# Operand splits in halves over six units, one transpose per unit, low parts of weights read back from DRAM

## The chip, the core and the metric

The kernel runs on one core of a Trainium2 chip. The metric is the device time of one execution in microseconds (us). Five engines work beside one another, each through its own instruction queue in order: TensorE (PE in the profile), VectorE (DVE), ScalarE (ACT), GpSimd (POOL) and SyncE (SP, which here only issues DMAs).

## What is computed

The reference is attention (8 heads, half with a local mask, half with a strided one), a top-2 mixture of experts, and a gated feed-forward block over 2304 tokens of width 512. The change touches the last block alone:

```
rms = sqrt(mean(x * x, axis=-1) + 1e-6)
xn  = x / rms * rms_g
g   = xn @ w_gate                      # 512 x 1536
out = (silu(g) * (xn @ w_val)) @ w_out # 1536 x 512
```

All of it is float32. The kernel makes a float32 product out of reduced-precision ones: an operand is split into a high part (a cast, on ACT) and a low part (operand minus high part, on DVE), and three matmuls are summed: high by high, high by low, low by high (`mm3`, lines 146 to 150).

## The kernel before

**Tiles and pairs.** The 2304 tokens are 18 tiles of 128 rows; six tiles make a pair p (two blocks of 384 tokens), so there are three pairs. The feed-forward width is cut into 12 columns f of 128. Columns 0 to 3 of pair 0 go through `plain` (line 1144) in a lead-in that a hand-written order at lines 1310 to 1361 sets. Everything else goes through `unit(n)` (line 1223), one for each (p, f): eight for pair 0 (f = 4 to 11), twelve for pair 1, twelve for pair 2.

**A unit** computes gate and value columns of both token blocks with seven block products (Strassen's scheme, Winograd's form) in place of eight. The seven activation operands A11, S2, S3, S1, A22, A12, S4 are split once per pair (`split_op`, line 1157); S1 to S4 are sums of blocks (`sums`, line 1164). The seven weight operands of a column lie in `uc` and `ud` in DRAM; `wload` (line 1176) loads those of unit n+2 and `wsplit` (line 1186) splits those of unit n+1, in four pieces, into the two halves of `BW`. TensorE's order within a unit is P1, P6, P7, P5, P4, P2, P3, each six matmuls of 384 columns, with the three output products `om` (three matmuls of 512 columns, line 1128) of each block of the unit before put between them. The products alternate between two PSUM banks (`nextb`, line 1117), so a product can't start before the product two places back has been read out: P1 by ACT's copy (line 1259), the others by DVE additions (lines 1265 to 1297). ACT does the silu (lines 1282, 1290) and the high part of h (line 1124), DVE the products and low parts.

**The next pair's tokens** come in while a pair runs. `fetch` (line 841) gathers the two expert rows of a tile on POOL's queue; `combine_parts` (line 849) gives four steps: weigh (ACT, line 855), add (DVE, line 858) with its square and sum (ACT, line 859), root (a tiny DVE step, line 862, and a power on POOL, line 863), and the normalising multiply (DVE, line 873). `tile_T` (line 1214) transposes the tile with four PE transposes (line 1219) into one of the two product banks, and ACT copies it to `xT` (line 1221). Lines 1227 and 1228 say in which unit a tile is fetched, combined and transposed: one or two tiles a unit, in units 3 to 8 or 4 to 9. A combine's steps stand behind P1, P6, P7 and P2; transposes stand before P5 and before P3. The sums S1 to S3 stand at the end of unit f = 9, S4 at the end of f = 10. `split_op` takes whole operands of 128x768, three in unit f = 10 and four in f = 11 (line 1245).

In each stage of a unit ACT's cast of a weight piece and DVE's subtraction that needs it are issued one behind the other (lines 1192 and 1193).

Of the kernel before, what the change touches and what calls it, by code (L numbers as in the profile page):

```python
# [9 lines left out]
F32 = mybir.dt.float32  # L10
# [14 lines left out]
def attn_moe_swiglu(ctx: ExitStack, tc: tile.TileContext, q, k, v, w_gate, w_noise, noise, w1, w2,  # L25
# [27 lines left out]
    yd = dram.tile([E * CAP + NOV * 128, DM], F32, name="yd")  # L53
    ud = dram.tile([18, 128, 1024], F32, name="ud")
    uc = dram.tile([NFC, 128, 1024], F32, name="uc")


    identf = keep.tile([128, 128], F32, name="identf")
# [782 lines left out]
    def fetch(t):  # L841
        YG[t] = []
        for kk in range(2):
            y = buf("yg")
            nc.gpsimd.indirect_dma_start(y, None, yd, bass.IndirectOffsetOnAxis(  # L845
                ap=posu[:, kk, t:t + 1], axis=0))
            YG[t].append(y)
# [19 lines left out]
    def combine(t):  # L867
        for part in combine_parts(t)[:3]:
            part()
# [258 lines left out]
    def om(p, f, i, t):  # L1128

        h = HG[p, f, i]  # L1130
        w = slot(cuse["O", f // 2])
        o = (f % 2) * 512
        b = ob[3 * i + t]
        mm3(b, h, w, (slice(t * 128, (t + 1) * 128),), (slice(o, o + 512),), f == 0, f == NFC - 1)
        if f == NFC - 1:
            y = buf("o")
            if t % 2 == 0:
                nc.scalar.copy(y, b)
            else:
                V.tensor_copy(y, b)  # L1140
            r = (p * 6 + i * 3 + t) * 128
            nc.sync.dma_start(out[r:r + 128, :], y)
# [11 lines left out]
        V.tensor_mul(sg, sg, pv_)  # L1154
        to_h(0, f, i, sg)()

    def split_op(p, n):
        src = {"A11": (0, 0), "A12": (0, 2), "A22": (1, 2)}.get(n)
        src = ST_[n] if src is None else xT[src[0]][:, src[1]:src[1] + 2]
        d = SOP[p, n]  # L1160
        nc.scalar.copy(d[:, 0], src)  # L1161
        V.tensor_tensor(d[:, 1], src, d[:, 0].bitcast(F32), op=OP.subtract)  # L1162

    def sums(*ns):
        a, b = xT
        a11, a12, a21, a22 = a[:, 0:2], a[:, 2:4], b[:, 0:2], b[:, 2:4]
        for n in ns:
            x, y, op = {"S1": (a21, a22, OP.add), "S2": (ST_["S1"], a11, OP.subtract),
                        "S3": (a11, a21, OP.subtract), "S4": (a12, ST_["S2"], OP.subtract)}[n]
            V.tensor_tensor(ST_[n], x, y, op=op)  # L1170


    cols = [(p, f) for p in range(NP) for f in range(NREG if p == 0 else 0, NFC)]
# [9 lines left out]
            nc.sync.dma_start(c, uc[f])  # L1183
            WS[n] = b, c

    def wsplit(n, i):
        if n < len(cols):
            d = BW[n % 2].rearrange("p s k n -> p s (k n)")
            b, c = WS[n]
            k0, k1, src = ((768, 1280, c[:, :512]), (0, 512, b[:, :512]), (1280, 1792, c[:, 512:]),  # L1190
                           (512, 768, b[:, 512:768]))[i]
            nc.scalar.copy(d[:, 0, k0:k1], src)  # L1192
            V.tensor_tensor(d[:, 1, k0:k1], src, d[:, 0, k0:k1].bitcast(F32), op=OP.subtract)  # L1193

    PROD = {"P1": ("A11", 0), "P2": ("A12", 1), "P3": ("S4", 2), "P4": ("A22", 6), "P5": ("S1", 5), "P6": ("S2", 3),
            "P7": ("S3", 4)}
# [17 lines left out]
    def tile_T(t):  # L1214
        ya, _ = X2.pop(t)
        turn["g"] += 1
        b = bank[(3, 6)[turn["g"] % 2]]
        for c in range(4):
            nc.tensor.transpose(b[:, c * 128:(c + 1) * 128], ya[:, c * 128:(c + 1) * 128], identf)
        o = (t % 3) * 128  # L1220
        nc.scalar.copy(xT[t // 3 % 2][:, :, o:o + 128], b.rearrange("p (c n) -> p c n", c=4))

    def unit(n):
        p, f = cols[n]
        pp_, pf = (p, f - 1) if f else (p - 1, NFC - 1)
        t6 = 6 * (p + 1)
        FETCH, COMB, TR = ({u: [k for k in range(6) if ([3, 3, 4, 5, 6, 7] if p else [4, 4, 5, 6, 6, 7])[k] + d == u] for u in range(NFC)}
                           if p + 1 < NP else {} for d in (0, 1, 2))
        trs = [t6 + k for k in TR.get(f, ())]
        wload(n + 2)  # L1230

        def om_(i, t):
            if (pp_, pf, i) in HG:
                om(pp_, pf, i, t)

        def tr():
            if trs:
                tile_T(trs.pop(0))

        def product(name):  # L1240
            b = nextb()
            prod(n, name, b)
            return b

        nxt = {NFC - 3: (), NFC - 2: ("A11", "S2", "S3"), NFC - 1: ("S1", "A22", "A12", "S4")}.get(f, ())
        nxt = [lambda x=x: split_op(p + 1, x) for x in nxt if p + 1 < NP]

        def next_op():
            if nxt:
                nxt.pop(0)()  # L1250

        cmb = [combine_parts(t6 + k) for k in COMB.get(f, ())]

        def comb():
            for c in cmb:
                c.pop(0)()

        b = product("P1")
        nc.scalar.copy(p1, b)
        comb()  # L1260
        LO.pop(0)()
        wsplit(n + 1, 0)
        om_(1, 0)
        b = product("P6")
        V.tensor_add(u2, b, p1)  # L1265
        wsplit(n + 1, 1)
        comb()
        om_(1, 1)
        b = product("P7")
        V.tensor_add(u3, b, u2)  # L1270
        wsplit(n + 1, 2)
        comb()
        om_(1, 2)
        tr()
        b = product("P5")
        V.tensor_add(sgb, b, u3)
        V.tensor_add(u2, b, u2)
        next_op()
        om_(0, 0)
        b = product("P4")  # L1280
        V.tensor_add(u3, b, u3)  # L1281
        nc.scalar.activation(u3, u3, AF.Silu)  # L1282
        wsplit(n + 1, 3)
        next_op()
        V.tensor_mul(sgb, sgb, u3)
        lo = to_h(p, f, 1, sgb)
        om_(0, 1)
        b = product("P2")
        V.tensor_add(sga, b, p1)
        nc.scalar.activation(sga, sga, AF.Silu)  # L1290
        lo()
        next_op()
        comb()
        om_(0, 2)
        tr()
        b = product("P3")
        V.tensor_add(u2, b, u2)  # L1297
        V.tensor_mul(sga, sga, u2)
        LO.append(to_h(p, f, 0, sga))
        next_op()  # L1300
        if p + 1 < NP:
            for k in FETCH.get(f, ()):
                fetch(t6 + k)
            if f == NFC - 3:
                sums("S1", "S2", "S3")
            if f == NFC - 2:
                sums("S4")


    advance(E * NF + 7)  # L1310
# [4 lines left out]
    plain(0, 1)  # L1315
    for t in range(3):
        om(0, 0, 0, t)
    plain(0, 2)
    combine(3)
    norm(3)  # L1320
    for t in range(3):
        om(0, 1, 0, t)
    combine(4)
    norm(4)
    plain(0, 3)
    x2_to_xt(3)
    combine(5)
    norm(5)
    for t in range(3):
        om(0, 2, 0, t)  # L1330
    x2_to_xt(4)
    om(0, 3, 0, 0)
    om(0, 3, 0, 1)
    x2_to_xt(5)
    om(0, 3, 0, 2)
    o_load(4)
    o_load(5)
    plain(1, 0)
    sums("S1", "S2")
    for h in range(2):  # L1340
        o_split(4, h)
    plain(1, 1)
# [1 line left out]
        o_split(5, h)  # L1344
    wload(0)
    wload(1)
    split_op(0, "S2")
    split_op(0, "S1")
    for t in range(3):
        om(0, 0, 1, t)  # L1350
    sums("S4", "S3")
    plain(1, 2)
    split_op(0, "S3")
    for t in range(3):
        om(0, 1, 1, t)
    for k in range(4):
        wsplit(0, k)
    plain(1, 3)
    split_op(0, "S4")
    for t in range(3):  # L1360
        om(0, 2, 1, t)
    LO = [lambda: None]
# [37 lines left out]
```

## Time and profile before

| | us |
|---|---|
| runs shown | 1126.36, 1126.59, 1130.0 |
| median | 1126.59 |
| profiled execution, time | 1129.92 |
| profiled execution, span of its trace | 1128.1 |

The profiled execution's own time is 1.8 us over its span, and 3.33 us over the median. Over the span PE is busy 94%, its weight loads 84%, DVE 66%, ACT 43%, POOL 20%; the 16 DMA engines move 148 GB/s on average. Attention and routing fill the first 200 us, the experts the time to 650 us, the lead-in of the last block 650 to 711 us, its units 711 to 1121 us. PE's busy time is to be read with care: matmuls overlap in the pipeline, and a matmul record of 384 columns lasts 0.34 us though the next one starts 0.17 us later.

### The profile page before, as it was taken

What the parts mean: (1) busy time and instruction counts of PE and PEld (TensorE: products, weight loads), DVE (VectorE), ACT (ScalarE), POOL (GpSimd) and SP (SyncE); (2) the same over time, 40 slices, a digit from 0 to 9 for tenths busy, and PEclk for the clock granted to TensorE, in tenths of its full rate; (3) what the DMA queues carried; (4) which work ended last, traced back from release to release, by engine and by line L of the source; (5) the groups of instructions that cost most, each with busy time, mean ns of one, the idle gap of its engine ahead of it and who ended that gap; (6) DMA issues with size and microseconds to landing.
All of it is one profiled execution on the core that took longest, in us unless ns stands there. A gap on an engine that the chain in (4) does not pass through costs nothing. (4 is left out here: it accounts for less than half of the span.)

```text
span 1128.1 us, 17700 instructions
## 1 busy us (share of the span) xinstructions
PE 1062.4 (94%) x6309; PEld 944.5 (84%) x6309; DVE 741.4 (66%) x1541; ACT 488.8 (43%) x1022; POOL 220.4 (20%) x261
## 2 busy tenths in 40 slices
PE   7988889999999999999999998989999999899998
PEld 5776767799999999988998897878889788799997
DVE  5675765358788888783552345666876767777675
ACT  4765752344444344432442334444444444443342
POOL 6555310303241414132100221021010110000000
PEclk8988989999999999999999998999999999999999
DMA  9967521468798899673641332232242332232211
GB/s 164 204 162 172 127 61 45 133 194 277 255 306 278 277 298 303 226 244 103 210 141 71 103 112 91 89 111 88 85 150 85 103 103 74 69 127 83 80 52 57
DMA packets 174810, 166.77 MB, mean 148 GB/s; under 512 B 66304, under 2 KB 134912, under 8 KB 174720
## 3 DMA queue, kind: packets, MB, share of 16 engines
q1 hardware_dynamic: 164656, 143.01, 40.9%
q0 software_dynamic: 9920, 22.35, 7.3%
q8 instruction: 50, 0.82, 0.3%
q14 instruction: 40, 0.33, 0.1%
q10 hardware_dynamic: 144, 0.26, 0.1%
HBM read 122.53 MB, written 42.99 MB: 147 GB/s over the span
## 5 line engine op out<-in xcount | busy, mean ns | idle before, releaser
L148 PE MATMUL bank<-xta,low 128*128 128x384 f32 x376 | 130.2, 346 | 12.0 <-DVE u L1270 4.2
L150 PE MATMUL bank<-xta,low 128*128 128x384 f32 x376 | 128.0, 340 | 0.0
L149 PE MATMUL bank<-xta,low 128*128 128x384 f32 x376 | 127.9, 340 | 0.0
L148 PE MATMUL bank<-ring,ha 128*128 128x512 f32 x288 | 114.6, 398 | 0.0
L150 PE MATMUL bank<-ring,ha 128*128 128x512 f32 x288 | 114.4, 397 | 0.0
L149 PE MATMUL bank<-ring,ha 128*128 128x512 f32 x288 | 114.2, 397 | 0.0
L148 PE MATMUL bank<-low 128*128 128x384 f32 x264 | 90.8, 344 | 10.8 <-DVE u L1270 4.3
L148 PEld LDWEIGHTS bank<-xta,low 128*128 128x128 f32 x376 | 71.8, 191 | 24.8 <-issue 6.9
L149 PE MATMUL bank<-low 128*128 128x384 f32 x264 | 89.9, 340 | 0.0
L150 PE MATMUL bank<-low 128*128 128x384 f32 x264 | 89.8, 340 | 0.0
L1029 POOL TENSOR_TENSOR dm<-dm,da 128x512 f32<-128x512 f32 x36 | 46.6, 1296 | 204.3 <-DVE da L1027 102.0
L161 ACT ACTIVATE ha<-bank 128x384 fp32r<-128x384 f32 x64 | 31.4, 490 | 123.1 <-PE bank L150 114.2
L162 DVE SCALAR_TENSOR_TENSOR ha<-bank,ha 128x384 fp32r<-128x384 f32 x64 | 35.5, 554 | 65.0 <-ACT ha L161 64.7
L149 PEld LDWEIGHTS bank<-xta,low 128*128 128x128 f32 x376 | 71.7, 191 | 4.3
L150 PEld LDWEIGHTS bank<-xta,low 128*128 128x128 f32 x376 | 71.5, 190 | 0.0
L1282 ACT ACTIVATE u<-u 128x384 f32<-128x384 f32 x32 | 16.8, 525 | 124.1 <-DVE u L1281 124.1
L148 PEld LDWEIGHTS bank<-low 128*128 128x128 f32 x264 | 49.6, 188 | 23.2 <-DVE u L1297 5.8
L845 POOL DMA_INDIRECT buf<-yd,posu x36 | 36.3, 1009 | 161.3 <-DMA yd<-buf 99.3
L150 PEld LDWEIGHTS bank<-ring,ha 128*128 128x128 f32 x288 | 54.1, 188 | 12.8 <-DVE ha L1126 0.6
L829 POOL DMA_INDIRECT buf<-xd,mapu x37 | 49.0, 1325 | 45.7 <-DVE posu L955 15.5
L148 PEld LDWEIGHTS bank<-ring,ha 128*128 128x128 f32 x288 | 54.2, 188 | 3.3 <-ACT ha L1124 0.5
L1193 DVE TENSOR_TENSOR low<-stage,low 128x512 fp32r<-128x512 f32 x64 | 39.5, 621 | 26.1 <-ACT low L1192 26.1
(284 smaller groups left out, 2828.9 us busy)
## 6 DMA issues: line engine op xcount, KB each, us to landing
stage<-in_moe_w_dram SPq DMA_DIRECT2D x128, 256.0 KB
yd<-buf SPq DMA_DIRECT2D x40, 256.0 KB
ud<-dm SPq DMA_DIRECT2D x36, 256.0 KB
stage<-uc SPq DMA_DIRECT2D x16, 512.0 KB
wc<-uc SPq DMA_DIRECT2D x16, 512.0 KB
yd<-zero SPq DMA_DIRECT2D x28, 256.0 KB
raw<-in_moe_w_gate_dram SPq DMA_DIRECT2D x12, 512.0 KB
raw<-in_moe_w_val_dram SPq DMA_DIRECT2D x12, 512.0 KB
```

Of the source, the lines that this page charges most:

```text
L148: nc.tensor.matmul(o, l[(slice(None), 0) + lsl], r[(slice(None), 0) + rsl], start=first, stop=False)
L149: nc.tensor.matmul(o, l[(slice(None), 0) + lsl], r[(slice(None), 1) + rsl], start=False, stop=False)
L150: nc.tensor.matmul(o, l[(slice(None), 1) + lsl], r[(slice(None), 0) + rsl], start=False, stop=last)
L161: nc.scalar.activation(h[:, 0], p, AF.Relu)
L162: nc.vector.scalar_tensor_tensor(h[:, 1], p, 0.0, h[:, 0].bitcast(F32), op0=OP.max, op1=OP.subtract)
L829: nc.gpsimd.indirect_dma_start(t, None, xd, bass.IndirectOffsetOnAxis(ap=mapu[:, e * NT + j:e * NT + j + 1], axis=0))
L845: nc.gpsimd.indirect_dma_start(y, None, yd, bass.IndirectOffsetOnAxis(ap=posu[:, kk, t:t + 1], axis=0))
L1029: nc.gpsimd.tensor_tensor(m, m, a.bitcast(F32), op=OP.add)
L1193: V.tensor_tensor(d[:, 1, k0:k1], src, d[:, 0, k0:k1].bitcast(F32), op=OP.subtract)
L1282: nc.scalar.activation(u3, u3, AF.Silu)
```

## The change

- `split_op` works on one half (128x384) and one part (high or low) at a time; `sums` works on a range of columns.
- `extras(p, f)` lays the next pair's splits and sums out over units f = 7 to 11 and f = 0 of the next pair. Within a unit they are taken one a stage, and a half's low part is issued one stage behind its high part.
- `wsplit` becomes `whi` and `wlo`. A piece's high part is cast one stage ahead of its subtraction; the first piece of unit n+2 is cast at the end of unit n.
- `wlo`: the first time that a column's weights are split, the low part (128x1792, 896 KB) is stored to a new DRAM tile `ul` by one DMA; in later pairs it is loaded from there by one DMA, and DVE does nothing for it. The columns 4 to 11 are stored in pair 0, 0 to 3 in pair 1: 12 stores, 20 loads.
- One tile a unit: fetched at f = 2 to 7, combined at f = 3 to 8, transposed at f = 4 to 9, with the transpose behind P1 and its `om`, before P6. The normalising multiply moves from behind P2 to behind P5.
- At the end of a pair other than the last, all six output copies are ACT's.
- In the lead-in, combines of tiles 3, 4 and 5 are moved forward and interleaved around `plain(0, 2)` and `plain(0, 3)`; fetches 6 and 7 and the combine of tile 6 are added to it.

```
+    ul = dram.tile([NFC, 128, 1792], F32, name="ul")
...
-            if t % 2 == 0:
+            if t % 2 == 0 or p + 1 < NP:
...
-    def split_op(p, n):
+    def split_op(p, n, h, part):
         src = {"A11": (0, 0), "A12": (0, 2), "A22": (1, 2)}.get(n)
-        src = ST_[n] if src is None else xT[src[0]][:, src[1]:src[1] + 2]
-        d = SOP[p, n]
-        nc.scalar.copy(d[:, 0], src)
-        V.tensor_tensor(d[:, 1], src, d[:, 0].bitcast(F32), op=OP.subtract)
-    def sums(*ns):
+        src = (ST_[n] if src is None else xT[src[0]][:, src[1]:src[1] + 2])[:, h]
+        d = SOP[p, n][:, :, h]
+        if part == 0:
+            nc.scalar.copy(d[:, 0], src)
+        else:
+            V.tensor_tensor(d[:, 1], src, d[:, 0].bitcast(F32), op=OP.subtract)
+    def sums(n, sl=slice(0, 384)):
         a, b = xT
-        a11, a12, a21, a22 = a[:, 0:2], a[:, 2:4], b[:, 0:2], b[:, 2:4]
-        for n in ns:
-            x, y, op = {"S1": (a21, a22, OP.add), "S2": (ST_["S1"], a11, OP.subtract),
-                        "S3": (a11, a21, OP.subtract), "S4": (a12, ST_["S2"], OP.subtract)}[n]
-            V.tensor_tensor(ST_[n], x, y, op=op)
+        a11, a12, a21, a22 = (x[:, c:c + 2, sl] for x in (a, b) for c in (0, 2))
+        x, y, op = {"S1": (a21, a22, OP.add), "S2": (ST_["S1"][:, :, sl], a11, OP.subtract),
+                    "S3": (a11, a21, OP.subtract), "S4": (a12, ST_["S2"][:, :, sl], OP.subtract)}[n]
+        V.tensor_tensor(ST_[n][:, :, sl], x, y, op=op)
...
-    def wsplit(n, i):
+    def whi(n, i):
-            k0, k1, src = ((768, 1280, c[:, :512]), (0, 512, b[:, :512]), (1280, 1792, c[:, 512:]),
-                           (512, 768, b[:, 512:768]))[i]
-            nc.scalar.copy(d[:, 0, k0:k1], src)
-            V.tensor_tensor(d[:, 1, k0:k1], src, d[:, 0, k0:k1].bitcast(F32), op=OP.subtract)
+            nc.scalar.copy(d[:, 0, slice(*PIECE[i])], (c[:, :512], b[:, :512], c[:, 512:], b[:, 512:768])[i])
+    def wlo(n, i):
+        if n < len(cols):
+            p, f = cols[n]
+            d = BW[n % 2].rearrange("p s k n -> p s (k n)")
+            b, c = WS[n]
+            sl = slice(*PIECE[i])
+            if (p and (p - 1, f) in cols):
+                if i == 0:
+                    nc.sync.dma_start(d[:, 1].bitcast(F32), ul[f])
+            else:
+                V.tensor_tensor(d[:, 1, sl], (c[:, :512], b[:, :512], c[:, 512:], b[:, 512:768])[i],
+                                d[:, 0, sl].bitcast(F32), op=OP.subtract)
+                if i == 3:
+                    nc.sync.dma_start(ul[f], d[:, 1].bitcast(F32))
...
+    def extras(p, f):
+        if p + 1 == NP:
+            return []
+        def halves(n):
+            return [(lambda h=h: split_op(p + 1, n, h, 0), lambda h=h: split_op(p + 1, n, h, 1)) for h in range(2)]
+        def part(n, k):
+            return None, lambda: sums(n, slice(k * 128, k * 128 + 128))
+        a11, s2, s3, s1, a22, a12, s4 = (halves(n) for n in ORDER)
+        s4s = [(None, lambda k=k: sums("S4", slice(k * 192, k * 192 + 192))) for k in range(2)]
+        return {7: [*a11, part("S1", 0), part("S2", 0), part("S3", 0)],
+                8: [part(n, 1) for n in ("S1", "S2", "S3")],
+                9: [part(n, 2) for n in ("S1", "S2", "S3")] + s2,
+                10: s3 + s4s, 11: s1 + a22 + [a12[0]], 12: [a12[1]] + s4}.get(f, [])
...
+        more = p + 1 < NP
+        ex = deque(extras(p, f) if f else extras(p - 1, NFC) if p else [])
+        todo = []
+        cmb = combine_parts(t6 + f - 3) if more and 3 <= f < 9 else []
...
+        def extra(k=1, last=False):
+            while todo:
+                todo.pop(0)()
+            for _ in range(0 if last else k):
+                if ex:
+                    hi, lo = ex.popleft()
+                    if hi is not None:
+                        hi()
+                    todo.append(lo)
...
         b = product("P1")
         nc.scalar.copy(p1, b)
         comb()
         LO.pop(0)()
-        wsplit(n + 1, 0)
+        wlo(n + 1, 0)
+        whi(n + 1, 1)
+        extra()
         om_(1, 0)
+        if more and 4 <= f < 10:
+            tile_T(t6 + f - 4)
         b = product("P6")
         V.tensor_add(u2, b, p1)
-        wsplit(n + 1, 1)
+        wlo(n + 1, 1)
+        whi(n + 1, 2)
         comb()
+        extra()
         om_(1, 1)
         b = product("P7")
         V.tensor_add(u3, b, u2)
-        wsplit(n + 1, 2)
+        wlo(n + 1, 2)
+        whi(n + 1, 3)
         comb()
+        extra()
         om_(1, 2)
-        tr()
         b = product("P5")
         V.tensor_add(sgb, b, u3)
         V.tensor_add(u2, b, u2)
-        next_op()
+        comb()
+        extra(2)
         om_(0, 0)
         b = product("P4")
         V.tensor_add(u3, b, u3)
         nc.scalar.activation(u3, u3, AF.Silu)
-        wsplit(n + 1, 3)
-        next_op()
+        wlo(n + 1, 3)
+        extra(last=True)
         V.tensor_mul(sgb, sgb, u3)
...
         V.tensor_add(sga, b, p1)
         nc.scalar.activation(sga, sga, AF.Silu)
         lo()
-        next_op()
-        comb()
         om_(0, 2)
-        tr()
         b = product("P3")
         V.tensor_add(u2, b, u2)
         V.tensor_mul(sga, sga, u2)
         LO.append(to_h(p, f, 0, sga))
-        next_op()
-        if p + 1 < NP:
-            for k in FETCH.get(f, ()):
-                fetch(t6 + k)
-            if f == NFC - 3:
-                sums("S1", "S2", "S3")
-            if f == NFC - 2:
-                sums("S4")
+        whi(n + 2, 0)
+        if more and 2 <= f < 8:
+            fetch(t6 + f - 2)
...
     for t in range(3):
         om(0, 0, 0, t)
-    plain(0, 2)
     combine(3)
     norm(3)
+    plain(0, 2)
+    c4, c5 = combine_parts(4), combine_parts(5)
+    c4.pop(0)()
+    c5.pop(0)()
+    c4.pop(0)()
+    x2_to_xt(3)
+    for c in (c5, c4, c5, c4, c5):
+        c.pop(0)()
     for t in range(3):
         om(0, 1, 0, t)
-    combine(4)
-    norm(4)
     plain(0, 3)
-    x2_to_xt(3)
-    combine(5)
-    norm(5)
+    x2_to_xt(4)
     for t in range(3):
         om(0, 2, 0, t)
-    x2_to_xt(4)
-    om(0, 3, 0, 0)
-    om(0, 3, 0, 1)
     x2_to_xt(5)
-    om(0, 3, 0, 2)
+    for t in range(3):
+        om(0, 3, 0, t)
     o_load(4)
     o_load(5)
+    fetch(6)
     plain(1, 0)
-    sums("S1", "S2")
+    sums("S1")
+    sums("S2")
     for h in range(2):
...
-    split_op(0, "S2")
-    split_op(0, "S1")
+    fetch(7)
+    for x in ("S2", "S1"):
+        for h in range(2):
+            for k in range(2):
+                split_op(0, x, h, k)
     for t in range(3):
         om(0, 0, 1, t)
-    sums("S4", "S3")
+    sums("S4")
+    sums("S3")
+    combine(6)
+    norm(6)
     plain(1, 2)
-    split_op(0, "S3")
+    for h in range(2):
+        for k in range(2):
+            split_op(0, "S3", h, k)
     for t in range(3):
         om(0, 1, 1, t)
-    for k in range(4):
-        wsplit(0, k)
+    for i in range(4):
+        whi(0, i)
+        wlo(0, i)
+    whi(1, 0)
     plain(1, 3)
-    split_op(0, "S4")
+    for h in range(2):
+        for k in range(2):
+            split_op(0, "S4", h, k)
     for t in range(3):
         om(0, 2, 1, t)
```

## Rows read from the trace of the kernel before

**Rows 1.** The page's first part: busy us, share of the span, instructions, by engine.
```profile
PE 1062.4 (94%) x6309; PEld 944.5 (84%) x6309; DVE 741.4 (66%) x1541; ACT 488.8 (43%) x1022; POOL 220.4 (20%) x261
```

**Rows 2.** ACT in order of time: P1's copy in nine units (start, length).
```profile
712.32 0.48 ACT L1259 COPY p<-bank 128x384 f32<-128x384 f32 x1 [1.24 <-PE bank L150]
...
723.81 0.48 ACT L1259 COPY p<-bank 128x384 f32<-128x384 f32 x1
...
796.22 0.47 ACT L1259 COPY p<-bank 128x384 f32<-128x384 f32 x1
...
825.61 0.47 ACT L1259 COPY p<-bank 128x384 f32<-128x384 f32 x1
...
871.73 0.48 ACT L1259 COPY p<-bank 128x384 f32<-128x384 f32 x1
...
952.74 0.47 ACT L1259 COPY p<-bank 128x384 f32<-128x384 f32 x1
...
982.36 0.47 ACT L1259 COPY p<-bank 128x384 f32<-128x384 f32 x1
...
1005.28 0.48 ACT L1259 COPY p<-bank 128x384 f32<-128x384 f32 x1
...
1016.88 0.48 ACT L1259 COPY p<-bank 128x384 f32<-128x384 f32 x1
```

**Rows 3.** PE's waits by releaser (us, times, longest): 712 to 826, then 826 to 983.
```profile
PE bank L148 <- DVE u L1270: 4.3, 4, 1.7
...
PE bank L148 <- DVE u L1270: 4.2, 5, 1.1
```

**Rows 4.** One combining unit of pair 1, by time: ACT, ACT, DVE, PE.
```profile
890.78 0.63 ACT L859 ACTIVATE buf<-buf 128x512 f32<-128x512 f32 x1 [2.01 <-issue]
...
891.41 0.60 ACT L1192 CAST low<-stage 128x512 fp32r<-128x512 f32 x1
...
892.05 0.69 DVE L1193 TENSOR_TENSOR low<-stage,low 128x512 fp32r<-128x512 f32 x1 [0.88 <-ACT low L1192]
...
891.22 0.44 PE L148 MATMUL bank<-xta,low 128*128 128x384 f32 x1 [1.07 <-DVE u L1270]
```

**Rows 5.** DVE groups from 712 to 1128: idle before them at the end.
```profile
L1126 DVE TENSOR_TENSOR ha<-sga,ha 128x384 fp32r<-128x384 f32 x32 | 17.8, 557 | 16.3 <-ACT ha L1124 16.2
L1162 DVE TENSOR_TENSOR xta<-sS,xta 128x768 fp32r<-128x768 f32 x5 | 4.8, 956 | 2.5 <-ACT xta L1161 2.5
```

**Rows 6.** The lead-in, DVE and PE: tile 5's normalising, its transposes, first unit.
```profile
682.43 0.75 DVE L873 SCALAR_TENSOR_TENSOR buf<-buf,ms,gB 128x512 f32<-128x512 f32 x1 [0.66 <-POOL ms L863]
...
683.23 0.66 PE L138 MATMUL bank<-identf,buf 128*128 128x128 f32 x4 [3.86 <-DVE buf L873]
...
711.05 0.33 PE L148 MATMUL bank<-xta,low 128*128 128x384 f32 x1
```

**Rows 7.** Windows: span, busy PE, PEld, DVE, ACT, POOL; clock; DMA share; GB/s.
```profile
689.00:691.00 2.00, 2.00 (x8) 2.00 (x8) 0.00 (x0) 0.49 (x1) 0.00 (x0) 0.50 0.31 104
...
871.73:952.74 81.01, 75.50 (x386) 66.55 (x385) 56.39 (x109) 36.16 (x80) 11.12 (x14) 1.00 0.29 95
...
1015.00:1016.00 1.00, 1.00 (x8) 1.00 (x7) 0.90 (x3) 0.02 (x1) 0.00 (x0) 1.00 0.95 349
1016.00:1017.00 1.00, 1.00 (x6) 0.86 (x6) 0.37 (x1) 0.54 (x2) 0.00 (x0) 1.00 0.64 229
```

**Rows 8.** PE in unit 9 of pair 1: a tile's four transposes, merged.
```profile
943.76 0.60 PE L1219 MATMUL bank<-identf,buf 128*128 128x128 f32 x4
```

**Rows 9.** Around P1's copy in a unit of pair 2: PE's first `om`, then ACT.
```profile
1004.39 0.39 PE L148 MATMUL bank<-ring,ha 128*128 128x512 f32 x1
...
1004.86 0.51 ACT L1124 CAST ha<-sga 128x384 fp32r<-128x384 f32 x1 [1.44 <-DVE sga L1298]
...
1005.65 0.62 ACT L1192 CAST low<-wc 128x512 fp32r<-128x512 f32 x1
```

**Rows 10.** SP's queue in time: the last weight load of a unit being issued.
```profile
1013.90 0.42 SPq L1183 DMA_DIRECT2D wc<-uc  x1
```

More of the change, by code (lines that the diff above doesn't have):

```diff
@@ L1184, in wload @@
             WS[n] = b, c
-    def wsplit(n, i):
+    PIECE = ((768, 1280), (0, 512), (1280, 1792), (512, 768))
+    def whi(n, i):
         if n < len(cols):
@@ L1226, in unit @@
         t6 = 6 * (p + 1)
-        FETCH, COMB, TR = ({u: [k for k in range(6) if ([3, 3, 4, 5, 6, 7] if p else [4, 4, 5, 6, 6, 7])[k] + d == u] for u in range(NFC)}
-                           if p + 1 < NP else {} for d in (0, 1, 2))
-        trs = [t6 + k for k in TR.get(f, ())]
+        more = p + 1 < NP
+        ex = deque(extras(p, f) if f else extras(p - 1, NFC) if p else [])
+        todo = []
+        cmb = combine_parts(t6 + f - 3) if more and 3 <= f < 9 else []
         wload(n + 2)
@@ L1234, in om_, with comb @@
                 om(pp_, pf, i, t)
-        def tr():
-            if trs:
-                tile_T(trs.pop(0))
+        def extra(k=1, last=False):
[7 more added lines that the diff above has]
+                    todo.append(lo)
+        def comb():
+            if cmb:
+                cmb.pop(0)()
         def product(name):
@@ L1243, in product @@
             return b
[L1245 to L1256, printed above, removed]
         b = product("P1")
```

## The prediction, made blind

> **What bounds it now.** I read the page's first part first: PE is busy 94% of the span [rows 1]. That is an average, and it says only that no other engine can be the bound for long. So I looked for the stretches in which PE is not paced by its own work, by taking P1's copy as a clock hand: its distance from one unit to the next is the length of a unit [rows 2]. In pair 2, where no next pair is prepared, a unit takes 1016.88 - 1005.28 = 11.60 us. Its matmuls move 42 x 384 + 18 x 512 = 25344 columns, so 0.458 ns a column; a product of six matmuls is then 1.06 us and one `om` 0.70. I take 11.60 as what PE alone costs.
>
> Against it, pair 0: the first unit (f = 4) 11.49, f = 5 to 9 together 72.41 (five units, 14.5 each), f = 10 and 11 29.39 (14.7 each). Pair 1: f = 0 to 3 46.12 (11.5 each), f = 4 to 9 81.01 (13.5 each), f = 10 and 11 29.62 (14.8 each) [rows 2]. So some 14 + 6 + 11 + 6 = 38 us lie over PE's pace, in just the units that prepare a pair, of which the transposes, priced below, are 12 x 0.60 = 7.2.
>
> The waits say why. The longest kind of PE wait in both pairs is for the DVE addition that reads P7, up to 1.7 us at a time [rows 3]. In a combining unit [rows 4] ACT sits for 2.01 us before the square, because that needs DVE's add; the cast of the third weight piece stands behind it in ACT's queue; DVE's subtraction of this piece then waits 0.88 us, and behind that stand the additions that free the banks. The reader should see a ring between two in-order queues, each waiting for the other within one stage. In f = 10 and 11 the whole-operand splits do the same: casts and subtractions of 128x768, the latter 0.96 us each [rows 5].
>
> [...]
>
> **The change, part by part.** Lead-in: tile 5's combine moves from behind `plain(0, 3)` to ahead of it. A `plain` is 24 x 384 columns, 4.2 us, more than the wait of 3.86; so the wait goes, and I take the clock's 3 us with it, as the clock fell behind that idle time alone: 6.9 us. Given back: the combine of tile 6 now stands in ACT's and DVE's queues ahead of `plain(1, 2)`'s multiply, which frees a bank; no row shows such a chain on the path there, so it costs between 0 (hidden by PE's work) and 4 us (all of its steps in series). One of its waits, 0.66 us for POOL [rows 6], is small, so I stay near the low end and take 1.2. **Lead-in: -5.7, bounds -7 to -2.5.**
>
> Units with a transpose: the ring is cut, since casts run one stage ahead of their subtractions and the square stands behind the next weight cast. DVE keeps up: it is busy 56.39 of 81.01 us in the worst stretch of pair 1 [rows 7], and from there on loses four subtractions a unit. What is new is the bank. With the transposes (0.60 us [rows 8]) behind P1, P6 takes P1's bank, not P3's, and must wait for P1's copy. In a clean unit [rows 2, 9] P1's slot ends at 1004.39 where `om` starts; ACT's cast of h follows at 1004.86 and the copy from 1005.28 to 1005.76, 1.37 behind P1. The change puts one more cast between them, the first weight piece of unit n+2: 0.62 long, 0.11 of it overlapped as for the copy (0.48 long, its successor 0.37 behind it). So the copy ends 1.88 behind P1. PE has 0.70 of `om` and 0.60 of transposes until then, 1.30: it waits 0.6, and 0.1 is lost as a matmul behind a wait lasts 0.44 [rows 4] in place of 0.34. I take 0.7 a unit; ends are 0 and 1.2 (the wait of 1.07 that such a unit has now [rows 4], and the restart). A unit with a transpose is 11.60 + 0.60 + 0.7 = 12.90. In f = 7 two casts of A11 stand ahead of ACT's copy of the transposes, which frees P7's bank: 0.3 more once a pair.
> Pair 0, f = 5 to 9: 5 x 12.90 + 0.3 = 64.8 against 72.41: **-7.6**. Pair 1, f = 4 to 9: 6 x 12.90 + 0.3 = 77.7 against 81.01: **-3.3**. Pair 0's f = 4 has half the `om` (20736 columns, 9.5 us) and is 2.0 over that now; it gains a transpose with its wait (1.3) and a combine, and I leave it at 11.5: **0**, bounds -1.5 to +1.5.
>
> Units f = 10 and 11: three and four operands of 128x768 become some five half-size pieces a unit, one a stage. Two halves cost DVE 2 x 0.56 against 0.96 [rows 5], 0.16 more for each of 14 operands, hidden in DVE's idle time. Nothing else is late there, and no transpose: 2 x 11.65 against 29.39 and 29.62, **-6.1 and -6.3**; at worst half of the excess stays, 6 us in all. The pieces that spill into f = 0, and the three output copies a pair that ACT takes from DVE, I cost at 0: ACT is busy 36.16 of 81.01 us [rows 7]; without that cover it is three copies of a 512-column bank, under 2 us a pair.
>
> Low parts in DRAM: 12 stores and 20 loads of 917 KB on SP's queue. A load for unit n+1 can't go before P3 of unit n-1 has read the buffer, and must be there for P1 of unit n+1, one unit later. The last weight DMA of a unit is issued at 1013.90 [rows 10]; its and its neighbour's 640 KB move at 349 and 229 GB/s and are through by 1017 [rows 7]. 917 KB at 229 GB/s are 4.0 us, about 5 from issue to landing; with the unit's 896 KB of other weight loads in the same stretch, 9. The unit hides either. The stores delay SP's next weight load to the last stages of the unit, still a unit ahead of its use. POOL's gathers are as many as before, one tile a unit. The normalising multiply now comes one product sooner behind POOL's power, 0 to 0.7 us a tile (the 0.66 above); I take 0, as two bank additions stand between. In pair 2 PE is already at its pace, so DVE's saved subtractions buy nothing: 0.
>
> Sum: -5.7 - 7.6 - 3.3 - 6.1 - 6.3 = -29.0. Against the profiled execution's own 1129.92 that is 1100.9. This execution is 3.33 over the median, and whether that excess is among the things that go isn't shown: with the median of 1126.59 the sum gives 1097.6. I forecast between them, **1099**.
>
> [...] PE now idles briefly at the same bank in 11 more or less equal units; the row of pair 1's f = 4 to 9, with waits of 1.07 in it, has the clock at 1.00 throughout [rows 7], so I cost the clock at nothing. [...]
>
> **Rivals.** *The bank wait doesn't appear*, since ACT gets to the copy sooner: 11 x 0.7 = 7.7 less, 1091. For it: ACT is mostly idle. Against: the cast of h before it waits for a DVE product that nothing moves. Chance 0.13.
> *Half the gain*: transposing units stay at 13.5 (11 x 0.6 = +6.6) and the lead-in gives only 2.5 (+3.2) because DVE, with two more steps in most stages, is late for P5's and P4's banks: 1109. For it: pair 0 still subtracts weights, and a stage gives 1.76 us. Chance 0.17.
> *Slower, low parts late*: P1 of each of 20 units waits for its load. Price: each us of landing over the 11.6 of a unit costs 20; it turns the result slower from 11.6 + 29/20 = 13.1 us on, and at 13.5 it costs 20 x 1.9 = 38, 9 more than the rest gives: 1136. For it: traffic of a unit doubles and the queue is in order. Against: 349 GB/s for a lone load [rows 7]. Chance 0.04.
> [...] Chance 0.02.
> *No effect*: the rings were not the cause, and what one engine no longer waits for the other does: 1127. Against: each wait in [rows 4] names its cause. Chance 0.03.
>
> **Numbers.** The forecast has 0.61. No change, within 0.3% (3.4 us, about what a measurement of this kernel can tell from none), has 0.03; slower 0.06; faster 0.61 + 0.13 + 0.17 = 0.91. The low end takes in most of the missing bank wait from the median, 1089; the high end the half gain and part of the bounds of f = 10 and 11, 1113. Outside is about 0.15.
>
> **What would show it.** Right: P1's copies 12.9 apart in transposing units and 11.6 to 11.7 in f = 10 and 11; a PE wait for ACT's P1 copy in each of the twelve transposing units, the largest kind that is left; no wait of 3.86 and clock 1.00 in the lead-in; the first unit's P1 near 705 where it is at 711.05 now [rows 6]; pair 2 at 11.60. Wrong: waits for the `ul` load, PE waits for DVE's additions of over 1 us, a clock of 0.50 among the units.

## The result, and the profile after

The changed kernel takes **1100.88 us** (median of four runs, 1100.13 to 1101.69); the kernel before, run beside it, 1126.92 (four runs, 1126.36 to 1130.0). The ratio is **0.9764 [0.9744, 0.9784]**. The forecast was 1099, range 1089 to 1113, with 0.91 on faster. The profiled execution took 1100.19, over a span of 1098.4.

The first part of the page after, to hold against [rows 1]:

```profile
PE 1051.4 (96%) x6309; PEld 944.9 (86%) x6309; DVE 700.1 (64%) x1489; ACT 494.5 (45%) x1044; POOL 223.1 (20%) x261
```

PE issues the same 6309 matmuls and is busy 11 us less, for the same work: a record behind a wait is longer (0.45 for 0.34, in the rows of E1 below), and so is one at a granted clock of 0.50 (0.52 for 0.34, from 687 to 691 us of the kernel before; 3.4 of the 11 us lie in the lead-in, in which PE was busy 52.18 and is now 48.81). So PE's busy time doesn't hold the answer; the distances between P1's copies do, as in [rows 2]. ACT after, in order of time:

```profile
704.61 0.47 ACT L1294 COPY p<-bank 128x384 f32<-128x384 f32 x1
...
716.85 0.47 ACT L1294 COPY p<-bank 128x384 f32<-128x384 f32 x1
729.79 0.47 ACT L1294 COPY p<-bank 128x384 f32<-128x384 f32 x1
742.74 0.47 ACT L1294 COPY p<-bank 128x384 f32<-128x384 f32 x1
...
781.83 0.47 ACT L1294 COPY p<-bank 128x384 f32<-128x384 f32 x1
...
851.42 0.47 ACT L1294 COPY p<-bank 128x384 f32<-128x384 f32 x1
...
929.33 0.47 ACT L1294 COPY p<-bank 128x384 f32<-128x384 f32 x1
940.93 0.47 ACT L1294 COPY p<-bank 128x384 f32<-128x384 f32 x1
952.52 0.47 ACT L1294 COPY p<-bank 128x384 f32<-128x384 f32 x1
```

P1's copies of units with a transpose are 12.94 and 12.95 apart (716.85, 729.79, 742.74), those of units f = 10 and 11 of pair 1 11.60 and 11.59. Before, units f = 5 to 8 of pair 0 and 4 to 8 of pair 1 took 13.6 to 17.7 (f = 9 12.1 and 11.7), units f = 10 and 11 14.3 to 15.4. From the first P1 copy to the last, over 31 units, the kernel before took 397.36 and the changed one 374.99: -22.4. The lead-in (its first plain silu to the first P1 copy) fell from 56.33 to 49.82: -6.5. Ahead of that, in code that the change doesn't touch, this execution is 1.2 shorter (654.79 against 655.98), and behind the last P1 copy 0.3 longer. Together -29.7, the difference of the two spans.

PE's waits after, 655 to 1099 us (us in all, times, longest):

```profile
PE bank L149 <- ACT p L1294: 7.2, 11, 0.8
PE bank L149 <- ACT u L1154: 0.7, 1, 0.7
```

The waits of [rows 3] for the addition that reads P7 are gone. What is left is mainly one kind: P6 waiting for P1's copy, eleven times, 0.65 each on the mean. That the ring is open is best seen on DVE. First the largest group of weight subtractions of the kernel before (704 to 1127 us), then the same group of the kernel after (704 to 1098); the last column is DVE's idle time just ahead of them and what ended it:

```profile
L1193 DVE TENSOR_TENSOR low<-stage,low 128x512 fp32r<-128x512 f32 x64 | 39.5, 621 | 26.1 <-ACT low L1192 26.1
```

```profile
L1208 DVE TENSOR_TENSOR low<-stage,low 128x512 fp32r<-128x512 f32 (+1 forms) x20 | 12.4, 620 | 0.0
```

Before, 26.1 us of DVE's idle time stood right in front of a subtraction of this group that waited for its own cast (with the other pieces it is 52.5); after, none in any group: the cast is a stage old. The instruction itself lasts 620 ns either way.

### The profile page after: what moved, and what is told of

Same layout as the page of the kernel before. It is cut to its first block, busy times and chain, and to the rows that moved or that the text cites. A ratio compares the mean times of both kernels' runs of the same rounds, so it can differ in the third digit from the quotient of the medians.

```text
span 1098.4 us, 17694 instructions
## 1 busy us (share of the span) xinstructions
PE 1051.4 (96%) x6309; PEld 944.9 (86%) x6309; DVE 700.1 (64%) x1489; ACT 494.5 (45%) x1044; POOL 223.1 (20%) x261
## 5 line engine op out<-in xcount | busy, mean ns | idle before, releaser
L846 POOL DMA_INDIRECT buf<-yd,posu x36 | 38.5, 1069 | 155.2 <-DMA yd<-buf 98.6
L151 PEld LDWEIGHTS bank<-ring,ha 128*128 128x128 f32 x288 | 54.0, 187 | 12.4 <-DVE ha L1127 0.3
L149 PEld LDWEIGHTS bank<-low 128*128 128x128 f32 x264 | 49.6, 188 | 15.7 <-ACT p L1294 9.8
L132 DVE TENSOR_TENSOR low<-stage,low 128x1024 fp32r<-128x1024 f32 x34 | 42.6, 1256 | 23.2 <-ACT low L131 21.4
```

The lines of the kernel that those rows point to most:

```text
L132: lo_engine.tensor_tensor(r[:, 1], st, r[:, 0].bitcast(F32), op=OP.subtract)
L149: nc.tensor.matmul(o, l[(slice(None), 0) + lsl], r[(slice(None), 0) + rsl], start=first, stop=False)
L151: nc.tensor.matmul(o, l[(slice(None), 1) + lsl], r[(slice(None), 0) + rsl], start=False, stop=last)
```

## The experiments

Each chip measured the kernel before anew (1122.87, 1125.89 and 1122.69 for the three groups that ran together), so kernels of different groups are compared by their ratios. "Units" is the time from the first P1 copy to the last in the profiled execution; it leaves out the first 650 us, which vary by up to 8 us from one profiled execution to another.

### E2: the low parts without DRAM

```diff
-            if (p and (p - 1, f) in cols):
-                if i == 0:
-                    nc.sync.dma_start(d[:, 1].bitcast(F32), ul[f])
-            else:
-                V.tensor_tensor(d[:, 1, sl], ...)
-                if i == 3:
-                    nc.sync.dma_start(ul[f], d[:, 1].bitcast(F32))
+            V.tensor_tensor(d[:, 1, sl], ...)
```

> The low parts of weights are made by DVE in every unit; the stores to ul and the loads from it are gone. Theory (DVE has room once casts run a stage ahead, so the DRAM copy buys nothing): 1100.9, units of pair 1 at 12.9 and 11.6 as now. Rival (DVE's 2.2 us a unit are needed in pair 1's units that prepare pair 2): those nine units are 0.3 to 1 us longer, 1104 to 1110.

Measured: 1097.2, ratio 0.976 [0.9735, 0.9785]; units 374.87 against 374.99. Part four of the change, 32 transfers of 896 KB, buys nothing here and costs nothing: DVE has room for all its subtractions once they need not wait. (At another place of the transposes it buys 2.2 us: E10.)

### E4: the ring closed again

E2's kernel with each cast back in the stage of its subtraction:

```diff
+        whi(n + 1, 0)
         wlo(n + 1, 0)
-        whi(n + 1, 1)
...
+        whi(n + 1, 1)
         wlo(n + 1, 1)
-        whi(n + 1, 2)
...
-        whi(n + 2, 0)
```

> Each weight piece is cast and subtracted in the same stage again, as before the change, DVE makes all low parts (no ul), and no cast stands ahead of P1's copy; transposes stay before P6, operands stay halved. Theory of the prediction (the ring of ACT and DVE within a stage was what made combining units long): the ten units with a combine are 13.2 us or longer although the bank wait is gone, the two with a transpose alone 12.4; 3 to 7 us slower than the changed kernel, ratio to the kernel before 0.979 to 0.983. Rival (the place of the transposes and their number a unit were the cause): all twelve at 12.3 to 12.5, 6 us faster, ratio 0.971.

Measured: 1108.96, ratio 0.9852 [0.9824, 0.9879]; units 384.02, 9.2 over E2. The size is above the 3 to 7 us that were expected, and it lies elsewhere. The ten units with a combine were to take 13.2 or longer; four do (f = 7 and 8, in which sums and splits share the queues), the other six are 12.83 to 12.88, no longer than the transposing units of the changed kernel, and f = 9, with a transpose alone, is 13.28 and not 12.4. Unit f = 3 of pair 1 shows the ring by itself, with a combine and no transpose: 12.87 where E2 has 11.59. ACT's P1 copies of f = 7 and 8 of pair 0, then those around f = 3 of pair 1, and PE's waits of 655 to 1140 us:

```profile
744.33 0.47 ACT L1287 COPY p<-bank 128x384 f32<-128x384 f32 x1
...
759.43 0.47 ACT L1287 COPY p<-bank 128x384 f32<-128x384 f32 x1
...
772.95 0.47 ACT L1287 COPY p<-bank 128x384 f32<-128x384 f32 x1
...
844.91 0.47 ACT L1287 COPY p<-bank 128x384 f32<-128x384 f32 x1
...
857.78 0.47 ACT L1287 COPY p<-bank 128x384 f32<-128x384 f32 x1
```

```profile
PE bank L148 <- ACT ha L1124: 7.2, 10, 1.4
PE bank L148 <- ACT p L1287: 3.7, 11, 0.4
```

Units f = 7 and 8 are 15.10 and 13.52. With one cast fewer ahead of P1's copy, the bank wait halves (3.7 us in all for 7.2), and that pays for part of the ring: what the changed kernel doesn't have is PE waiting for ACT's cast of h, late behind the weight casts. So the two parts of the change pull against each other at this place, which led to the next two.

### E1: the extra cast ahead of P1's copy moved away

```diff
         nc.scalar.activation(sga, sga, AF.Silu)
+        whi(n + 2, 0)
         lo()
...
         LO.append(to_h(p, f, 0, sga))
-        whi(n + 2, 0)
```

> The first weight piece of unit n+2 is cast behind the second silu, ahead of the cast of h, in place of behind it; nothing else differs. Theory (P6 waits for its bank because this cast delays P1's copy by 0.52 us): the copy ends 1.37 us behind P1 and not 1.89, the PE wait for it shrinks from about 0.6 to 0.1 us, a transposing unit goes from 12.94 to 12.4 us, twelve of them give 6.5 us: 1094.4. Rival (the copy waits for the chain of DVE and ACT steps of h in any case, or DVE is what paces these units): 12.9 stays, 1100.9.

Measured: 1090.45, ratio 0.9708 [0.9683, 0.9732]; units 369.64, 5.35 less. Transposing units are 12.42 to 12.43, three of them 12.68 to 12.71. ACT and PE around P6 in the changed kernel:

```profile
728.85 0.51 ACT L1125 CAST ha<-sga 128x384 fp32r<-128x384 f32 x1 [1.95 <-DVE sga L1338]
729.27 0.61 ACT L1195 CAST low<-wc 128x512 fp32r<-128x512 f32 x1
729.79 0.47 ACT L1294 COPY p<-bank 128x384 f32<-128x384 f32 x1
...
729.08 0.60 PE L1237 MATMUL bank<-identf,buf 128*128 128x128 f32 x4
730.31 0.45 PE L149 MATMUL bank<-low 128*128 128x384 f32 x1 [0.64 <-ACT p L1294]
```

and in E1:

```profile
724.28 0.51 ACT L1125 CAST ha<-sga 128x384 fp32r<-128x384 f32 x1 [1.73 <-DVE sga L1339]
724.70 0.47 ACT L1294 COPY p<-bank 128x384 f32<-128x384 f32 x1
...
724.23 0.60 PE L1237 MATMUL bank<-identf,buf 128*128 128x128 f32 x4
725.23 0.44 PE L149 MATMUL bank<-low 128*128 128x384 f32 x1 [0.40 <-ACT p L1294]
```

With the cast between them gone, the copy starts 0.42 behind the cast of h (724.28, 724.70) in place of 0.94 (728.85, 729.79), and a unit is 0.5 shorter. The prediction's bank wait is shown by its cause. It isn't gone: the copy still ends after the transposes.

### E5: the transposes ahead of P5

```diff
-        if more and 4 <= f < 10:
-            tile_T(t6 + f - 4)
         b = product("P6")
...
         om_(1, 2)
+        if more and 4 <= f < 10:
+            tile_T(t6 + f - 4)
         b = product("P5")
```

The sums and halves that need a tile begin two stages later.

> The transposes stand before P5 again (one tile a unit), and the sums and splits are moved on by up to two stages so that they stay behind them. Theory (before, P5 waited there because DVE was late with P7 through the ring with ACT; with the casts a stage ahead it is in time, and P6 no longer shares P1's bank): no bank wait, 12.3 us a transposing unit, 7 us less: 1094. Rival (the place itself costs the wait, whatever DVE does): 13.3 to 13.6 a unit, 1106 to 1109.

Measured: 1087.3, ratio **0.9686 [0.9655, 0.9718]**; units 366.48, 8.5 less than in the changed kernel. Three P1 copies of pair 1, and PE's longest kind of wait from 690 to 1090 us:

```profile
844.21 0.47 ACT L1295 COPY p<-bank 128x384 f32<-128x384 f32 x1
...
856.25 0.46 ACT L1295 COPY p<-bank 128x384 f32<-128x384 f32 x1
...
868.28 0.47 ACT L1295 COPY p<-bank 128x384 f32<-128x384 f32 x1
```

```profile
PE bank L149 <- DVE u L1310: 0.8, 2, 0.6
```

12.04 and 12.03 a unit (in pair 0 mostly 12.4: see E10): the transposes cost 0.44 over the 11.60 of a unit without them, and the wait for P1's copy is gone from the list. The place that the kernel before had, ahead of P5, is the better one once the ring is cut; what it is worth with the ring closed is the next question.

### E10 and E11: is it the place or the ring?

E10 is E5 without the low parts in DRAM (E2's edit); E11 is E10 with casts and subtractions in one stage (E4's edit).

> Transposes before P5 with casts a stage ahead, and DVE makes all low parts (no ul). In the run with ul, pair 0's combining units (DVE subtracts there) took 12.4 and pair 1's (it doesn't) 12.04. Theory (that 0.37 is DVE's subtractions, hidden behind the bank wait in the changed kernel): pair 1's five combining units go to 12.4, 2 us more than with ul. Rival (pair 0's excess comes from something else, such as the stores): pair 1 stays at 12.04.

> As the run before it, but with the transposes before P5, where they stood before the change (one tile a unit): against the run with transposes before P5 and casts a stage ahead (12.0 to 12.4 a unit) it differs in the weights' casts and in ul alone. Theory (ring): the wait for P7's addition is back, 13.3 to 13.6 in the ten combining units, as units f = 6 to 8 had before the change; about 10 us slower than that run, ratio 0.977 or so. Rival (one tile a unit and halved operands are enough): 12.5 or less, ratio 0.970.

Measured: E10 1093.73, ratio 0.9711 [0.9682, 0.974]; E11 1107.72, ratio 0.9832 [0.9802, 0.9862]. With E2 and E4 they fill a square, all without the low parts in DRAM (units, us):

| | cast one stage ahead | cast in its stage |
|---|---|---|
| transposes ahead of P6 | 374.87 (E2) | 384.02 (E4) |
| transposes ahead of P5 | 368.69 (E10) | 384.36 (E11) |

With the ring closed the place is worth nothing (0.3); with it open, ahead of P5 is 6.2 better. Cutting the ring is worth 9.2 at P6 and 15.7 at P5. PE's waits of E11, 655 us to the end, show the ring as [rows 3] did:

```profile
PE bank L148 <- DVE u L1303: 7.8, 9, 1.1
PE bank L148 <- DVE sga L1327: 3.3, 6, 0.9
```

In E10 the first of these is 1.4 us in all. E11's size was not foreseen: the loss is 14 to 16 us and not 10, and the units aren't all 13.3 to 13.6, but 12.9 where a combine stands without sums and splits, and 14.7 and 13.8 in f = 7 and 8. The rival is right for a part, too: with the ring closed E11's units still take 13.0 us less than those of the kernel before (397.36). And ACT, ACT, DVE in a combining unit of E11:

```profile
720.68 0.63 ACT L859 ACTIVATE buf<-buf 128x512 f32<-128x512 f32 x1 [2.02 <-issue]
721.31 0.60 ACT L1194 CAST low<-stage 128x512 fp32r<-128x512 f32 x1
...
721.94 0.69 DVE L1203 TENSOR_TENSOR low<-stage,low 128x512 fp32r<-128x512 f32 x1 [0.88 <-ACT low L1194]
```

ACT's 2.02 ahead of the square and DVE's 0.88 ahead of the subtraction are those of [rows 4] within 0.01. For ACT's wait both profiles name only "issue"; that it was for DVE's add follows from the times (here the add ends at 720.59, the square starts at 720.68; 890.70 and 890.78 before). So the reading of the ring from the trace of before stands. E5 against E10 (366.48, 368.69) gives the low parts in DRAM 2.2 us at this place, in pair 1, whose units are 12.04 with them and 12.40 without.

### E9: both edits

E5 with E1's move of the cast.

> Transposes before P5, and the first weight piece of unit n+2 cast behind the second silu (both edits together). Theory (with the transposes before P5, P1's copy holds up no bank; P6's addition needs the copy, which is 0.5 us earlier, and that helps DVE where it is late): pair 0's combining units 12.04 to 12.3 in place of 12.4, pair 1's 12.04 as they are; 0 to 1.5 us less than with the first edit alone. Rival (the early cast delays the cast of h, and with it DVE): 1 to 3 us more.

Measured: 1090.86, ratio 0.9693 [0.9663, 0.9723]; units 364.75, 1.7 less than in E5, a little over the 0 to 1.5 foreseen. The times don't separate E9 from E5, nor E1; all three beat both kernels. By its units E9 is the best.

### E3: whole operands split in f = 10 and 11

```diff
+    def split_whole(p, n):
+        ...
+        nc.scalar.copy(d[:, 0], src)
+        V.tensor_tensor(d[:, 1], src, d[:, 0].bitcast(F32), op=OP.subtract)
...
+        nxt = {NFC - 2: ("A11", "S2", "S3"), NFC - 1: ("S1", "A22", "A12", "S4")}.get(f, ())
```

> The seven operands are split whole (128x768, cast and subtraction back to back) in units f = 10 and 11 again, and S4 is summed whole at the end of f = 10; the weights' casts stay one stage ahead and the transposes where they are. Theory (the whole splits are what made f = 10 and 11 14.2 to 15.4 us long): 6.2 us a pair come back in full or for the most part, 1109 to 1113, with f = 10 and 11 at 14 to 15 us. Rival (the weights' casts and subtractions in one stage were the cause): 12 us or less for these units, 1103 at most.

Measured: 1105.29, ratio 0.9841 [0.9815, 0.9867]; units 384.25, 9.3 over the changed kernel. Two P1 copies around unit f = 10 of pair 1, and DVE inside it:

```profile
929.52 0.47 ACT L1307 COPY p<-bank 128x384 f32<-128x384 f32 x1
...
943.57 0.47 ACT L1307 COPY p<-bank 128x384 f32<-128x384 f32 x1
```

```profile
937.26 0.96 DVE L1247 TENSOR_TENSOR xta<-sS,xta 128x768 fp32r<-128x768 f32 x1 [1.31 <-ACT xta L1246]
...
940.50 0.96 DVE L1247 TENSOR_TENSOR xta<-sS,xta 128x768 fp32r<-128x768 f32 x1 [0.59 <-ACT xta L1246]
```

14.04 and 14.34 for f = 10 and 11 of both pairs where the halves give 11.60: the old way of splitting brings most of the old excess back although the weights' casts stay ahead. Three things go back together here: the size of a piece, a cast and its subtraction in one stage, and all seven operands in two units. Which of them counts most isn't separated; DVE waits 0.59 and 1.31 for the whole cast and then works 0.96. And f = 7 is 12.92 here like its neighbours, 13.22 in the changed kernel: its surplus of 0.3 is from A11's halves.

### E6: the old lead-in

```diff
+    plain(0, 2)
     combine(3)
     norm(3)
-    plain(0, 2)
-    c4, c5 = combine_parts(4), combine_parts(5)
...
+    combine(4)
+    norm(4)
     plain(0, 3)
+    x2_to_xt(3)
+    combine(5)
+    norm(5)
```

> The lead-in's combines of tiles 3, 4 and 5 and their transposes stand in the order of the kernel before; fetches 6 and 7, the combine of tile 6 and all units are as changed. Theory (tile 5's late combine costs 3.86 us of idle PE and some 3 us of lower clock): both are back, 6 to 7.5 us slower than the changed kernel, ratio 0.982, clock 0.50 for some 6 us behind the idle time. Rival (the idle time is there but the clock doesn't fall, or falls elsewhere anyway): 3 to 4 us, ratio 0.979.

Measured: 1102.98, ratio 0.9816 [0.9791, 0.984]; lead-in 56.03 in place of 49.82, units 374.96 as in the changed kernel. PE at tile 5's transposes, then windows of 2 us (span, busy PE, PEld, DVE, ACT, POOL; clock; DMA share; GB/s):

```profile
678.74 1.11 PE L139 MATMUL bank<-identf,buf 128*128 128x128 f32 x4 [3.86 <-DVE buf L874]
```

```profile
676.00:678.00 2.00, 0.00 (x0) 0.00 (x0) 0.50 (x3) 1.19 (x3) 0.55 (x1) 0.70 0.00 0
678.00:680.00 2.00, 1.26 (x5) 1.25 (x6) 1.29 (x2) 0.68 (x2) 1.63 (x2) 0.50 0.04 8
680.00:682.00 2.00, 2.00 (x6) 1.38 (x5) 0.69 (x1) 1.06 (x2) 1.70 (x2) 0.50 0.72 162
682.00:684.00 2.00, 2.00 (x9) 2.00 (x8) 0.00 (x0) 0.00 (x0) 1.01 (x2) 0.60 0.65 211
```

The wait is 3.86 again, to the hundredth, and the clock falls with it (0.70, then 0.50; in the changed kernel, without the wait, it is 1.00 from 673 to 679 us): wait and clock come and go as one here, 6.2 us together. The four windows, if the clock was either 1.00 or 0.50 within each, put the low clock at an estimated 6.8 us, from 676.8 to 683.6; PE still waits in the first 1.9 of them, so it is slowed for 4.9 us only.

### E8: the load of the low parts three times over

Each load is issued three times into the same place, so that its last copy lands two transfers later.

```diff
                     nc.sync.dma_start(d[:, 1].bitcast(F32), ul[f])
+                    nc.sync.dma_start(d[:, 1].bitcast(F32), ul[f])
+                    nc.sync.dma_start(d[:, 1].bitcast(F32), ul[f])
```

> Each low part is loaded from ul three times into the same place, one load behind the other, so it lands three times as late. Theory (one load lands in some 4 to 5 us and the unit has 11.6): three take 12 to 15 us, and units that load become 0 to 4 us longer: between 0 and 70 us slower, with PE waiting for the load; the excess a unit, plus 11.6, divided by three is the landing time. Rival (landing takes 10 us or more beside the other traffic, and the changed kernel was near its edge): units of 30 us, 300 us slower.

Measured: 1154.17, ratio 1.0277 [1.0252, 1.0302]; units 433.26, those that load 13.6 to 18.4. SP's queue, then PE's longest kind of wait, 655 us to the end:

```profile
1003.60 0.32 SPq L1207 DMA_DIRECT2D low<-ul  x1
1008.12 0.32 SPq L1208 DMA_DIRECT2D low<-ul  x1
```

```profile
PE bank L151 <- DMA low<-ul: 41.2, 17, 4.4
```

Three loads in a row make PE wait for DMA, so this chain sets the unit when it is long enough; from its second issue to its third are 4.5 us. From the first, which stands right behind the unit's other weight loads here (996.17 in this unit), to the second are 7.4. A unit of pair 2 is then 15.0 on the mean, 5.0 for each of three loads. In the changed kernel, where the load is issued ahead of the others, one load (4.5 to 5.0) is hidden more than twice over by 11.60; even behind them it would have an estimated 4 us to spare (11.60 - 7.4).

## Why the prediction was right, point by point

Each term of its sum beside the two profiled executions (us):

| | predicted | measured |
|---|---|---|
| lead-in | -5.7 | -6.5 |
| pair 0, f = 4 | 0 | +0.7 |
| pair 0, f = 5 to 9 | -7.6 | -7.4 |
| pair 1, f = 0 to 3 | 0 | +0.3 |
| pair 1, f = 4 to 9 | -3.3 | -3.1 |
| pair 0, f = 10 and 11 | -6.1 | -6.2 |
| pair 1, f = 10 and 11 | -6.3 | -6.4 |
| pair 2 and the end | 0 | +0.1 |
| ahead of the lead-in | 0 | -1.2 |
| sum | -29.0 | -29.7 |

- **The ring as a cause of the long units**: shown by E4 and E11, worth 9 us at the place that the change gives the transposes and 16 ahead of P5. It isn't the whole cause that the prediction made of it. With the ring closed, pair 1's f = 4 to 9 take 80.5 (E4) and 80.0 (E11), near the 81.0 before; but pair 0's f = 5 to 9 take 67.7 and 66.8 of 72.4 before (65.0 in the changed kernel). So some 5 of the 7.4 that pair 0 gains come without cutting the ring.
- **A term that the prediction left out** is part of the rest of pair 0's gain: the clock. It had the clock fall behind the lead-in's wait alone. In the kernel before it also fell in pair 0's f = 7, the unit of 17.73, behind two waits, of 0.57 ahead of the transposes and 1.73 behind them (PE's row; then windows, columns as in [rows 7]):

```profile
758.90 0.44 PE L148 MATMUL bank<-low 128*128 128x384 f32 x1 [1.73 <-DVE u L1270]
```

```profile
759.00:760.00 1.00, 1.00 (x5) 1.00 (x6) 0.27 (x1) 1.00 (x4) 0.00 (x0) 0.72 0.00 0
...
761.00:762.00 1.00, 1.00 (x4) 0.81 (x3) 0.81 (x2) 0.00 (x0) 0.83 (x3) 0.50 0.42 145
```

  It was low for 3.4 us with PE busy, so an estimated 1.7 us, half of that, of pair 0's 7.4 are the clock's. The other 3 to 4 come with one tile a unit and the other parts of the change, which no run separates. That the term of 7.6 came out is partly luck.
- **The bank wait of P6 behind the transposes**: shown by E1, and by E5, where it is gone. But the 12.90 was right by two errors that cancel. The prediction put the transposes at their record's 0.60 and the wait at 0.70. E5 gives 12.04 - 11.60 = 0.44 for the transposes alone, so, if they cost the same at both places, the wait with its restart costs 12.94 - 12.04 = 0.90, within the bounds of 0 and 1.2. The wait was foreseen in twelve units and stands in eleven: pair 0's f = 4 has none.
- **The rival without this wait (1091)** is not what the change does, but it is what E5 and E9 are: 0.9686 and 0.9693 of 1126.92 are 1091.5 and 1092.3 on the scale of this measurement.
- **f = 7's 0.3**: 0.28 measured, gone in E3, where A11's halves are gone too, as foreseen.
- **f = 10 and 11**: 11.60 as foreseen; E3 shows that the new way of splitting does it, and E4 that the weights' ring has little part in it (24.1 us for both units with it closed, 23.2 open, 29.4 and 29.6 before).
- **Pair 0's f = 4** was costed at 0 and lost 0.7. Most of that is the copy by which units are timed, and not PE: at the end of this unit P1's copy stands later behind P1, by the cast put ahead of it. In E1 and E9, where that cast is away, the unit is 11.74 and 11.66; in E5, which has no bank wait, it is 12.21 like the 12.24 of the changed kernel. PE itself takes 10.79 from the start of one P1 (703.29, below) to that of the next, against 10.54 before (711.05 in [rows 6] and 721.59):

```profile
714.08 0.45 PE L149 MATMUL bank<-xta,low 128*128 128x384 f32 x1 [0.30 <-DVE sga L1332]
```

  So PE lost 0.25, with the transposes in it.
- **The lead-in** was mis-sized by 0.8, in two terms. No run shows the 3 us for the clock in its 6.9. What the trace of the kernel before shows (columns as in [rows 7]) is a low clock of 6.8 us, 684.4 to 691.2 if it was either 1.00 or 0.50 within each window:

```profile
683.00:685.00 2.00, 1.51 (x8) 0.94 (x8) 0.86 (x3) 1.07 (x2) 1.69 (x2) 0.84 0.26 37
685.00:687.00 2.00, 1.96 (x5) 1.56 (x6) 0.61 (x1) 0.59 (x1) 1.39 (x3) 0.50 0.67 207
687.00:689.00 2.00, 2.00 (x7) 2.00 (x7) 0.00 (x0) 0.00 (x0) 0.80 (x1) 0.50 0.65 184
...
691.00:693.00 2.00, 2.00 (x13) 2.00 (x12) 0.45 (x1) 0.00 (x0) 0.00 (x0) 0.95 0.00 0
```

  PE was at work for nearly all of it, so it cost an estimated 3.4, half of its length (by the distances of records of 384 columns, 0.32 us in it and 0.17 behind it, 3.2). What is given back was put at 1.2 and is 0.73, one matmul's wait for ACT's silu, late behind tile 6's square. With the wait of 3.86 that is 3.86 + 3.4 - 0.73 = 6.5, as measured. E6 brings back only 6.2, since 1.9 us of its low clock fall into the wait. PE in the changed kernel:

```profile
676.77 0.60 PE L139 MATMUL bank<-identf,buf 128*128 128x128 f32 x4
...
696.94 0.45 PE L149 MATMUL bank<-xta,low 128*128 128x384 f32 x1 [0.73 <-ACT u L1154]
...
703.29 0.33 PE L149 MATMUL bank<-xta,low 128*128 128x384 f32 x1
```

  Tile 5's transposes have no wait, and the first P1 is at 703.29 (711.05 in [rows 6], near 705 foreseen).
- **Low parts in DRAM at 0**: shown by E2, and E8 shows the margin; the rival of late loads falls.
- **Clock**: the row that answers to [rows 7], pair 1's f = 4 to 9 after (columns as there):

```profile
851.42:929.33 77.91, 74.16 (x385) 67.55 (x386) 47.42 (x95) 36.94 (x81) 12.77 (x13) 1.00 0.51 169
```

  Six waits at the same bank, one a unit, and the clock is 1.00; pair 0's f = 5 to 9 read 1.00 as well. So idle times of 0.65 us on the mean, every 12.9, left it there, and nothing for the clock was the right cost in the changed kernel's units. In the kernel before the clock did fall once among the units, to 0.50 in pair 0's f = 7 above; the prediction's row was of pair 1 alone.
- **Between profiled execution and median**: the sum against the profiled execution, 1100.9, met the median of 1100.88; the step down to 1099 was away from it. That is partly luck. The medians are 26.0 apart where the sum is 29.0 and the spans 29.7, and 1.2 of the spans' difference arose ahead of all changed code. Where the other 2.5 lay isn't settled.

**Still open.** Why PE takes 10.81 from P1 to P1 in pair 0's f = 4 even in E9, 0.9 over its pace of 9.5 and 0.44 for the transposes, wasn't tried; a wait of 0.3 for DVE's sga is part of it. What one tile a unit is worth by itself, and which part of the new splitting counts, no run separates. Whether E9 is faster than E5 by more than its units' 1.7 the times can't tell.

## What to carry to other kernels

When one engine's result feeds the next engine's work within a stage, and both queues run in order, move the producer one stage ahead before looking for work to remove: here that was worth 9 to 16 us, while removing 80 subtractions was worth 0 to 2. Two cures can fight: after cutting a ring, try the old place of whatever was moved along with it, since here the new place had come to cost 6 to 9 us. Where units are timed by one recurring instruction, check that it stands at the same distance behind PE's work at both ends. Cost an insertion between two users of a rotating buffer by who frees its buffer now, and by what stands ahead of that one in its queue.

## What the runs showed of the hardware that was not expected

A group of four 128-column transposes has a record of 0.60 us, yet lengthens a unit by only 0.44 (E5): here the record's length was more than the cost. And the drop of the clock to 0.50 with the single idle time of 3.86 in the lead-in came back with it in E6, whereas 0.65 us of idle time in each of eleven units left the clock at 1.00. Between the two lies the unit f = 7 of the kernel before: waits of 0.57 and 1.73 close behind one another, then 3.4 us at 0.50.
